# A head's first probability tile is transposed together with its second

## The chip, the cores and the metric

The kernel runs on one core of one Trainium2 chip. The metric is device time in microseconds (us) of one execution. Engines are called as in the profile: PE is TensorE's matmuls and PEld its weight loads, DVE is VectorE, ACT is ScalarE, POOL is GpSimd, SP is SyncE, which issues most DMAs.

## What is computed

Causal attention with a decay (4 batches, 8 heads, 576 rows, head size 64), then a small dense layer with a maximum over three products (moe1), then a routed layer of 8 experts, two per row. The change touches the attention alone:

```python
scores = scale * np.matmul(q, k.transpose(0, 1, 3, 2))
decay = cum[:, :, :, None] - cum[:, :, None, :]
scores = np.where(causal, -1000000000.0, scores + decay)
attn = np.exp(scores - np.max(scores, axis=-1, keepdims=True))
attn = attn / (np.sum(attn, axis=-1, keepdims=True) + 1e-09)
x = np.matmul(attn, v)
```

## The kernel before

Attention is cut into units: a batch's first 256 query rows (a short unit, tiles 0 and 1 of 128 rows) or its other 320 (a long unit, tiles 2, 3 and 4; tile 4 has 64 rows). A unit has 8 heads. The list `jobs` (lines 395 to 411) holds the 160 tiles in order: two per head in short units, three in long ones, there in the order 2, 4, 3 for heads of even number and 2, 3, 4 for odd ones. A tile is marked `first` or `last` within its head. The first 16 heads (a short and a long unit) are `plain`: their probabilities are used in one part. All later ones are split into a high and a low part, so that fp32 products can be made from faster ones.

A tile goes through these steps, each a function called from the loop in `attention()` (line 570): scores on TensorE (`st_S`, L446 or L448 and L449), mask, maximum and row minimum on VectorE (`st_max`, L457), exponential on ScalarE (`st_exp`, L462), division by the sum on VectorE and GpSimd (`st_norm`, L467, L468, L470), transposes on TensorE, one per 128 columns (`st_T`, L477), evacuation of the high part on ScalarE (`st_evac`, L489 or L503) and of the low part on VectorE (`st_evac2`, L510), and per head the product with V on TensorE (`st_pv`, L531 or L535) and its read-out (`st_x`, L547, or L550 and L551).

The loop is a pipeline written out by hand. Slot n has two halves. The first issues for ScalarE and VectorE: the evacuation of tile n-4, the exponential of n-1, the division of n-2, the maximum of n, the low part of n-4, the read-out of the head that ended with n-5. The second issues for TensorE: transposes of tile n-3, scores of tile n+1, the product with V of the head that ended with n-4. Engines run their queues in the order of issue, so this is the order of the work on each.

Between halves `att_to` (line 647) hands over to moe1 of the unit before: 22 groups a unit, of 12 or 18 matmuls (L661 to L663), whose results ScalarE and VectorE evacuate too (L681, L683, L687, L691, L712). These matmuls are what TensorE does while ScalarE and VectorE work on a tile. In the first unit, up to about 59 us, there are none yet. `post` (L730 to L856) routes the rows of a unit that moe1 is through with. After the last unit, from about 560 us, only the experts remain.

Buffers near the change: the transposes write to the PSUM tag `pt`, of which there are two; in long units the head's product with V takes its output `o` from the same two. Scores lie in `sA` (even tiles) or `sB` (odd ones, and the 64-row tile), one buffer each. Probabilities `P` are a ring of four.

Of the kernel before, what the change touches and what calls it, by code (L numbers as in the profile page):

```python
# [55 lines left out]
def moe_stack(ctx, tc, qk, v, f, w1, w2, w3, wo, wg, noise, e1, e2, out):  # L56
# [28 lines left out]
    with tc.manual_schedule():  # L85
# [113 lines left out]
        def load_v(b, ph, h):  # L199
            if hidx[b, ph, h] < H:  # L200
                if h % 2 == 0:
                    load_v_first(h)
                return
            vr = ap_.tile([128, 320], F32, tag="vr", name="vr", bufs=2).rearrange("p (j c) -> p j c", j=5)
            nj = 2 if ph == 0 else 4
            vh = v[b, :, h * D:(h + 1) * D]
            nc.sync.dma_start(vr[:, 0:nj, :], vh[0:nj * 128].rearrange("(j p) d -> p j d", p=128))
            if ph:
                nc.sync.dma_start(vr[0:64, 4, :], vh[512:576])
            vraws[b, ph, h] = vr  # L210
# [47 lines left out]
        def prep_v2(b, ph, h):  # L258
            if hidx[b, ph, h] < NV:
                return  # L260
            vr = vraws.pop((b, ph, h))
            s, pieces = v_pieces(b, ph, h)
            for pp, jj in pieces:
                nc.gpsimd.tensor_tensor(V[s][pp, jj, 64:128], vr[pp, jj, :],
                                        V[s][pp, jj, 0:64].bitcast(F32), op=OP.subtract)
# [130 lines left out]
        for b, ph in UNITS:  # L396
            for h in range(H):
                tiles = (0, 1) if ph == 0 else ((2, 4, 3) if h % 2 == 0 else (2, 3, 4))
                for n, i in enumerate(tiles):
                    t = Tile_()  # L400
# [50 lines left out]
        def st_max(t):  # L451
            st = ap_.tile([128, 4], F32, tag="stat", name="stat", bufs=6)
            t.st = st
            mk = maskw[0:t.w, MASK0 + t.w - t.kn:MASK0 + t.w]
            if t.i == 4:
                mk = mk.rearrange("p (a c) -> p a c", a=2)
            nc.vector.tensor_tensor_reduce(out=t.view, in0=t.view, in1=mk, scale=1.0, scalar=3.0e38,  # L457
                                           op0=OP.add, op1=OP.min, accum_out=st[0:t.w, 0:1])

        def st_exp(t):  # L460
            st = t.st
            nc.scalar.activation(t.pview, t.view, AF.Exp, bias=st[0:t.w, 0:1], scale=-1.0,  # L462
                                 accum_out=st[0:t.w, 1:2])

        def st_norm(t):
            st = t.st
            nc.vector.tensor_scalar(st[0:t.w, 2:3], st[0:t.w, 1:2], 1.0e-9, None, op0=OP.add)  # L467
            nc.vector.reciprocal(st[0:t.w, 3:4], st[0:t.w, 2:3])  # L468
            p = P[t.n % NP][0:t.w, 0:t.kn]
            nc.gpsimd.tensor_scalar(p, p, st[0:t.w, 3:4], 0.0, op0=OP.mult, op1=OP.add)  # L470

        def st_T(t):
            nb = t.i + 1
            p = P[t.n % NP]
            t.pt = ps_a.tile([128, 512], F32, tag="pt", name="pt", bufs=2)
            for j in range(nb):
                nc.tensor.transpose(t.pt[:, j * t.w:(j + 1) * t.w], p[0:t.w, j * 128:(j + 1) * 128],  # L477
                                    ident[0:t.w, 0:t.w])

        def st_evac(t):  # L480
            nb = t.i + 1
            hd = heads[t.b, t.ph, t.h]
            t.pl = None
            if t.plain:
                if t.first:
                    x = PT[t.h % 2]
                    hd["pf"] = x.rearrange("p (j c) -> p j c", j=5) if t.ph else \
                        x[:, 0:2 * QA_N].rearrange("p (j c) -> p j c", j=2)
                nc.scalar.activation(hd["pf"][:, 0:nb, t.c0:t.c0 + t.w],  # L489
                                     t.pt[:, 0:nb * t.w].rearrange("p (j c) -> p j c", j=nb), AF.Copy)  # L490
                return
            if t.first:
                if PT[0].dtype != F32R:
                    PT[:] = [ap_.tile([128, 5 * QB_N], F32R, tag=x, name=x) for x in ("PTh", "PTl")]
                if t.ph == 0:
                    o_ = (t.h % 2) * 2 * QA_N
                    hd["pt"] = [x[:, o_:o_ + 2 * QA_N].rearrange("p (j c) -> p j c", j=2) for x in PT]
                else:
                    hd["pt"] = [x.rearrange("p (j c) -> p j c", j=5) for x in PT]
            src = t.pt[:, 0:nb * t.w].rearrange("p (j c) -> p j c", j=nb)  # L500
            hh = hd["pt"][0][:, 0:nb, t.c0:t.c0 + t.w]
            ll = hd["pt"][1][:, 0:nb, t.c0:t.c0 + t.w]
            nc.scalar.activation(hh, src, AF.Copy)  # L503
            t.pl = (ll, src, hh)

        def st_evac2(t):
            if not t.pl:
                return
            ll, src, hh = t.pl
            nc.vector.tensor_tensor(ll, src, hh.bitcast(F32), op=OP.subtract)  # L510
# [27 lines left out]
        def st_x(t):  # L538
            hd = heads[t.b, t.ph, t.h]
            qn = SPAN[t.ph][1]  # L540
            o = hd["o"]
            r = (t.h % 2) * 64
            if r == 0:
                xf[0] = ap_.tile([128, QB_N], F32, tag="xf", name="xf")
            t.xf = xf[0]
            if t.plain:
                nc.scalar.activation(t.xf[r:r + 64, 0:qn], o[0:64, 0:qn], AF.Copy)  # L547
                return
            oc = ap_.tile([64, QB_N], F32, tag="oc", name="oc")
            nc.scalar.activation(oc[:, 0:qn], o[64:128, 0:qn], AF.Copy)  # L550
            nc.vector.tensor_tensor(t.xf[r:r + 64, 0:qn], o[0:64, 0:qn], oc[:, 0:qn], op=OP.add)  # L551
# [8 lines left out]
        def st_xl(t):  # L560
            if t.h % 2:
                qn = SPAN[t.ph][1]
                u, c = UNITS.index((t.b, t.ph)), t.h // 2
                XL[u, c] = mp.tile([128, QB_N], F32R, tag="xl", name="xl", bufs=XBUF)
                nc.gpsimd.tensor_tensor(XL[u, c][:, 0:qn], t.xf[:, 0:qn], XH[u, c][:, 0:qn].bitcast(F32),
                                        op=OP.subtract)
# [3 lines left out]
        def attention():  # L570
            NJ = len(jobs)

            def job(n):
                return jobs[n] if 0 <= n < NJ else None

            def nxt(t, d):
                k = hidx[t.b, t.ph, t.h] + d
                return hkey[k] if k < len(hkey) else None

            st_S(jobs[0])  # L580
            for n in range(NJT):
                now, last = job(n), lambda d: job(n - d) if job(n - d) and job(n - d).last else None
                if job(n - 4):
                    st_evac(job(n - 4))
                if job(n - 1):
                    st_exp(job(n - 1))
                if job(n - 2):
                    st_norm(job(n - 2))
                if now:
                    st_max(now)  # L590
                if job(n - 4):
                    st_evac2(job(n - 4))
                if last(6):
                    st_xl(last(6))
                if last(5):
                    st_x(last(5))
                tv = job(n - 3 - VSH)
                if tv and tv.first:
                    prep_v2(tv.b, tv.ph, tv.h)
                    k = nxt(tv, 2)  # L600
                    if k and (hidx[k] < H or hidx[k] >= NV + 2):
                        load_v(*k)
                yield
                if now and now.first and n and nxt(now, 1):
                    prep_head2(*nxt(now, 1))
                    k = hidx[now.b, now.ph, now.h]
                    if H <= k + AH < H + 3:
                        load_head(*hkey[k + AH])
                    if H + 3 <= k + 3 < len(hkey):
                        load_head(*hkey[k + 3])  # L610
                if job(n + 1) and job(n + 1).first and nxt(job(n + 1), 1):
                    prep_head(*nxt(job(n + 1), 1))
                tv = job(n - 2 - VSH)
                if tv and tv.first:
                    prep_v(tv.b, tv.ph, tv.h)
                if last(5):
                    st_xh(last(5))
                if job(n - 3):
                    st_T(job(n - 3))
                if job(n + 1):  # L620
                    st_S(job(n + 1))
                if last(4):
                    st_pv(last(4))
                    k = nxt(last(4), 2)
                    if k and H <= hidx[k] < NV + 2:
                        load_v(*k)
                yield
# [381 lines left out]
        n = 0  # L1009
# [233 lines left out]
```

## Time and profile before

| | |
|---|---|
| median of 3 runs | 1053.16 us (1051.28 to 1053.35) |
| profiled execution | 1053.1 us, span 1051.4 us |
| granted TensorE clock, mean | 0.995 |
| TensorE busy | 1010.5 us, 96% |
| VectorE busy | 537.7 us, 51% |
| ScalarE busy | 520.8 us, 50% |
| GpSimd busy | 487.9 us, 46% |
| probability transposes (L477) | 480, 76.7 us busy |

Busy time is from the page of the profile. TensorE's matmuls are pipelined and overlap, so its busy time isn't its time at full rate. What one costs is read from the starts of two that follow each other. In the timeline a row gives start, duration, engine, line, what is written and read, the count of merged instructions, and in brackets the idle time of the engine before it with what ended it.

### The profile page before, as it was taken

The numbers are of one execution on the slowest core, as the hardware profiler recorded it, in microseconds if no ns is written. First come the engines' busy times: TensorE is split into PE (matmuls) and PEld (weight loads), VectorE is DVE, ScalarE is ACT, GpSimd is POOL, SyncE is SP. The second block draws the span as 40 slices with busy tenths as digits, with TensorE's granted clock in tenths as the row PEclk, the third lists the DMA queues.
The fourth block names the chain that finished last, engine by engine and source line by source line (L and its number), as shares of the span: only waits on it lengthen the run. The fifth ranks groups of instructions, "written<-read, shape, count | busy, mean of one in ns | idle before, by whom it ended". The sixth has DMA issues, their size and how long they took to land.

```text
span 1051.4 us, 18712 instructions
## 1 busy us (share of the span) xinstructions
PE 1010.5 (96%) x6452; PEld 907.2 (86%) x6452; DVE 537.7 (51%) x1666; ACT 520.8 (50%) x1310; POOL 487.9 (46%) x573
## 2 busy tenths in 40 slices
PE   5899999999999999999999999999999999999996
PEld 3477798999989999999998889899898989898995
DVE  6989767587685876858363434222232322232210
ACT  5866766576665776666324244333333333333311
POOL 5766645545555555454345354443334342434202
PEclk9999999999999999999999999999999999999999
DMA  6875344332432213311025265543536353544203
GB/s 195 207 180 156 106 131 114 84 99 82 136 87 49 70 52 96 89 37 38 1 83 169 57 169 162 127 107 113 116 131 122 109 124 97 134 109 125 35 9 44
DMA packets 79728, 109.17 MB, mean 104 GB/s; under 512 B 37172, under 2 KB 43700, under 8 KB 79564
## 3 DMA queue, kind: packets, MB, share of 16 engines
q1 hardware_dynamic: 69388, 86.90, 28.8%
q0 software_dynamic: 10240, 21.02, 10.9%
q8 instruction: 53, 0.87, 0.4%
q14 instruction: 47, 0.39, 0.1%
HBM read 86.48 MB, written 21.39 MB: 103 GB/s over the span
## 4 chain that ended last, share of the span: by engine, by line
PE 78%; DVE 9%; DMA 5%; issue 3%; POOL 2%; ACT 2%; SPq 1%; POOLq 0%; DVEq 0%; ACTq 0%
PE m L661 8%; PE m L662 7%; PE m L663 7%; PE g L661 7%; PE g L662 7%; PE g L663 7%; PE m L974 6%; PE m L973 6%; PE m L972 6%; PE pt L477 4%; PE o L535 3%; PE o L531 2%; PE m L730 2%; PE t L938 2%; PE sB L448 1%
## 5 line engine op out<-in xcount | busy, mean ns | idle before, releaser
L470 POOL TENSOR_SCALAR P<-P,stat 128x512 f32<-128x512 f32 (+4 forms) x160 | 92.7, 579 | 206.4 <-DVE stat L468 117.3
L661 PE MATMUL g<-xTh,eh 128*128 128x384 f32 (+1 forms) x512 | 159.3, 311 | 0.6 <-DVE hl L957 0.6
L662 PE MATMUL g<-xTl,eh 128*128 128x384 f32 (+1 forms) x512 | 158.0, 309 | 0.0
L663 PE MATMUL g<-xTh,el 128*128 128x384 f32 (+1 forms) x512 | 157.9, 308 | 0.0
L979 POOL DMA_INDIRECT out_rows<-ys,dst x40 | 63.1, 1578 | 176.8 <-ACT ys L978 143.6
L309 POOL TENSOR_TENSOR el<-ew,eh 128x1024 fp32r<-128x1024 f32 x36 | 92.1, 2563 | 109.4 <-ACT eh L308 109.2
L957 DVE SCALAR_TENSOR_TENSOR hl<-g,hh 128x384 fp32r<-128x384 f32 (+1 forms) x120 | 58.2, 486 | 130.0 <-ACT hh L956 125.3
L972 PE MATMUL m<-eh,hh 128*128 128x512 f32 x296 | 118.8, 401 | 0.0
L974 PE MATMUL m<-eh,hl 128*128 128x512 f32 x296 | 117.1, 396 | 0.0
L956 ACT ACTIVATE hh<-g 128x384 fp32r<-128x384 f32 (+1 forms) x120 | 52.1, 435 | 130.9 <-PE g L663 130.6
L973 PE MATMUL m<-el,hh 128*128 128x512 f32 x296 | 116.8, 394 | 0.0
L941 DVE TENSOR_TENSOR xTl<-t,xTh 128x512 fp32r<-128x512 f32 x40 | 27.7, 692 | 157.1 <-ACT xTh L940 157.1
L978 ACT ACTIVATE ys<-m,mv 128x512 f32<-128x512 f32 x40 | 27.6, 689 | 161.1 <-issue 118.7
L661 PEld LDWEIGHTS g<-xTh,eh 128*128 128x128 f32 x512 | 96.7, 189 | 1.6 <-DVE hl L957 1.0
L662 PEld LDWEIGHTS g<-xTl,eh 128*128 128x128 f32 x512 | 96.8, 189 | 0.2 <-DVE xTl L941 0.2
L663 PEld LDWEIGHTS g<-xTh,el 128*128 128x128 f32 x512 | 96.7, 189 | 0.0
L503 ACT ACTIVATE PTh<-pt 128x128 fp32r<-128x128 f32 (+2 forms) x120 | 52.3, 436 | 77.7 <-PE pt L477 47.0
L477 PE MATMUL pt<-ident,P 128*128 128x128 f32 x480 | 76.7, 269 | 6.2 <-POOL P L470 4.6
L308 ACT ACTIVATE eh<-ew 128x1024 fp32r<-128x1024 f32 x64 | 67.4, 1055 | 8.5 <-DMA ew<-in_e 8.5
L974 PEld LDWEIGHTS m<-eh,hl 128*128 128x128 f32 x296 | 55.6, 188 | 13.2
L477 PEld LDWEIGHTS pt<-ident,P 128*128 128x128 f32 x480 | 53.0, 143 | 15.9 <-POOL P L470 8.8
L973 PEld LDWEIGHTS m<-el,hh 128*128 128x128 f32 x296 | 55.7, 188 | 11.9
(312 smaller groups left out, 2891.3 us busy)
## 6 DMA issues: line engine op xcount, KB each, us to landing
ew<-in_e SPq DMA_DIRECT2D x64, 512.0 KB
qkraw<-in_qk SPq DMA_DIRECT2D x64, 224.0 KB
wr<-in_w SPq DMA_DIRECT2D x18, 512.0 KB
qkraw<-in_qk SPq DMA_DIRECT2D x48, 128.0 KB
out_rows<-zt SPq DMA_DIRECT2D x19, 256.0 KB
vr<-in_v SPq DMA_DIRECT2D x37, 128.0 KB
x2d<-row SPq DMA_DIRECT2D x16, 256.0 KB
vr<-in_v SPq DMA_DIRECT2D x24, 64.0 KB
```

The source lines that it names most:

```text
L308: nc.scalar.activation(hi_, raw, AF.Copy)
L309: leng.tensor_tensor(lo_, raw, hi_.bitcast(F32), op=OP.subtract)
L470: nc.gpsimd.tensor_scalar(p, p, st[0:t.w, 3:4], 0.0, op0=OP.mult, op1=OP.add)
L477: nc.tensor.transpose(t.pt[:, j * t.w:(j + 1) * t.w], p[0:t.w, j * 128:(j + 1) * 128], ident[0:t.w, 0:t.w])
L661: nc.tensor.matmul(o, lh, rh, start=first, stop=False)
L662: nc.tensor.matmul(o, lh, rl, start=False, stop=False)
L663: nc.tensor.matmul(o, ll, rh, start=False, stop=last)
L957: nc.vector.scalar_tensor_tensor(hl, o, 0.0, hh.bitcast(F32), op0=OP.max, op1=OP.subtract)
L972: nc.tensor.matmul(y, hh, wh[:, f_ % 2, :], start=(f_ == 0), stop=False)
L973: nc.tensor.matmul(y, hh, wl[:, f_ % 2, :], start=False, stop=False)
L974: nc.tensor.matmul(y, hl, wh[:, f_ % 2, :], start=False, stop=(f_ == 7))
L979: nc.gpsimd.indirect_dma_start(out=out[:, :], out_offset=bass.IndirectOffsetOnAxis(ap=ex["dst"][:, e, c:c + 1], axis=0), in_=ys, in_offset ...
```

## The change

In the loop of `attention()` a head's first tile is transposed one slot later, in the slot of its second tile and right ahead of it. Its two evacuations are moved by one slot as well, so that both tiles of the pair are evacuated in the same half slot, the first one first: both high parts ahead of the exponential, both low parts behind the maximum. Third tiles, and the product with V, stay in their slots. Nothing else is changed.

```diff
                 now, last = job(n), lambda d: job(n - d) if job(n - d) and job(n - d).last else None
-                if job(n - 4):
-                    st_evac(job(n - 4))
+                turned = [t for t, d in ((job(n - 5), 5), (job(n - 4), 4)) if t and t.first == (d == 5)]
+                for t in turned:
+                    st_evac(t)
                 if job(n - 1):
                     st_exp(job(n - 1))
                 if job(n - 2):
                     st_norm(job(n - 2))
                 if now:
                     st_max(now)
-                if job(n - 4):
-                    st_evac2(job(n - 4))
+                for t in turned:
+                    st_evac2(t)
...
-                if job(n - 3):
-                    st_T(job(n - 3))
+                for t, d in ((job(n - 4), 4), (job(n - 3), 3)):
+                    if t and t.first == (d == 4):
+                        st_T(t)
                 if job(n + 1):
                     st_S(job(n + 1))
```

## Rows read from the trace of the kernel before

**Rows 1.** The page, busy time, share of the span and instructions of TensorE.
```profile
PE 1010.5 (96%) x6452; PEld 907.2 (86%) x6452; DVE 537.7 (51%) x1666; ACT 520.8 (50%) x1310; POOL 487.9 (46%) x573
```

**Rows 2.** Waits of TensorE: who waited for whom, us in total, times, longest.
```profile
PE pt L477 <- POOL P L470: 4.6, 3, 2.1
...
PE pt L477 <- DVE PTl L510: 1.5, 3, 0.6
...
PE sB L448 <- DVE xf L551: 1.4, 3, 0.5
```

**Rows 3.** Timeline of TensorE around runs of three and four 128-row transposes.
```profile
203.96 0.28 PE L663 MATMUL m<-xh,w00l 128*128 128x256 f32 x1
204.08 0.49 PE L477 MATMUL pt<-ident,P 128*128 128x128 f32 x3
204.32 0.37 PE L448 MATMUL sB<-QKB 128*64 128x288 f32 x1
204.54 0.29 PE L449 MATMUL sB<-QKA 128*64 128x288 f32 x1
204.67 0.29 PE L448 MATMUL sB<-QKB 128*64 128x288 f32 x1
...
210.05 0.60 PE L477 MATMUL pt<-ident,P 128*128 128x128 f32 x4
```

**Rows 4.** Timeline of TensorE where transposes of a 64-row tile begin.
```profile
218.93 0.28 PE L663 MATMUL m<-xh,w10l 128*128 128x256 f32 x1
219.13 0.52 PE L477 MATMUL pt<-ident,P 64*128 64x64 f32 x5
```

**Rows 5.** Timeline of TensorE at its idle times in the first long unit.
```profile
44.49 0.55 PE L477 MATMUL pt<-ident,P 128*128 128x128 f32 x3 [0.86 <-POOL P L470]
45.19 0.50 PE L448 MATMUL sA<-QKB 128*128 128x512 f32 x1 [0.15 <-ACT P L462]
...
49.96 0.37 PE L477 MATMUL pt<-ident,P 128*128 128x128 f32 x1 [2.12 <-POOL P L470]
```

**Rows 6.** Timeline of all engines ahead of a third tile's transposes, a later long unit.
```profile
220.47 0.76 DVE L457 CUSTOM_DVE_ANT_0 sB<-sB,maskw 64x576 f32<-64x576 f32 x1 [1.14 <-PE sB L449]
...
221.16 0.48 DVE L510 TENSOR_TENSOR PTl<-pt,PTh 128x320 fp32r<-128x320 f32 x1
...
221.58 0.38 PE L477 MATMUL pt<-ident,P 128*128 128x128 f32 x2
```

**Rows 7.** Timeline of all engines where a second tile's transposes wait.
```profile
227.78 0.54 DVE L510 TENSOR_TENSOR PTl<-pt,PTh 128x384 fp32r<-128x384 f32 x1
...
228.47 0.52 PE L477 MATMUL pt<-ident,P 128*128 128x128 f32 x3 [0.56 <-DVE PTl L510]
```

**Rows 8.** Timeline of all engines in a short unit, sixth head.
```profile
157.07 0.37 ACT L503 ACTIVATE PTh<-pt 128x256 fp32r<-128x256 f32 x1
...
157.48 0.27 PE L477 MATMUL pt<-ident,P 128*128 128x128 f32 x1
...
157.58 0.21 ACT L462 ACTIVATION_READ_ACCUMULATOR P<-sA,stat 128x1 f32 x1
...
157.84 0.45 PE L448 MATMUL sA<-QKB 128*128 128x384 f32 x1
```

**Rows 9.** Timeline where the product with V waits, seventh and first head.
```profile
165.02 0.41 DVE L510 TENSOR_TENSOR PTl<-pt,PTh 128x256 fp32r<-128x256 f32 x1
...
165.58 0.36 PE L535 MATMUL o<-PTh,V 128*128 128x256 f32 x1 [1.10 <-DVE PTl L510]
...
257.18 0.19 PEld L535 LDWEIGHTS o<-PTl,V 128*128 128x128 f32 x1 [0.23 <-DVE PTl L510]
```

**Rows 10.** Windows: busy us of PE, PEld, DVE, ACT, POOL, clock, DMA share, GB/s.
```profile
49.00:50.00 1.00, 0.04 (x1) 0.04 (x1) 1.00 (x4) 0.41 (x1) 0.81 (x2) 1.00 1.43 140
50.00:57.00 7.00, 6.14 (x19) 3.69 (x20) 6.80 (x18) 4.35 (x12) 5.32 (x6) 0.51 0.49 104
```

## The prediction, made before the changed kernel ran

> **What bounds the kernel now.** First the page: TensorE (PE) is busy 96% of the span and the next engine half of it, so the time is the length of TensorE's instruction stream plus its idle time [rows 1]. Next the view of waits, for TensorE alone, because a change of order can act only on what a view of waits shows or on what it newly creates: all of TensorE's waits for probabilities (pt from POOL) come to 4.6 us in three places [rows 2], so no more than that can be won by transposing a first tile later. Then the timeline of TensorE around a transpose run, to price the run itself [rows 3, 4], and the timeline of all engines at the places where the moved work stands close behind something [rows 5 to 9]. Last the clock by windows [rows 10].
>
> In what follows a head's tiles are its first, second and (in long units) third, and "slot" is one turn of the attention loop. The profiled execution took 1053.1 us (span 1051.4), the median of the runs is 1053.16, so sums are made on 1053.1.
>
> **The runs themselves.** The change removes no instruction. All 480 transposes stay; 64 heads have one run less each. What a run costs beyond its transposes: a run of three is shown with 0.49 us, a run of four with 0.60, so one transpose is 0.11 us. Three are 0.33, yet the score matmul behind them starts after 0.24 (204.08 to 204.32), 0.09 early. That score matmul takes 0.22 (204.32 to 204.54) against 0.13 for the next of the same form (204.54 to 204.67), 0.09 more: the two cancel. Before the run the last MoE matmul gives way after 0.12 us (203.96 to 204.08), which is its ordinary pitch [rows 3]. So a run of 128-row transposes costs its transposes and nothing for beginning or ending, and joining two runs saves about 0. The 64-row tile is different: the matmul before it gives way after 0.20 us (218.93 to 219.13), 0.08 more [rows 4]. In the 16 long heads with even number this tile now follows the first tile's transposes instead of a MoE matmul. No row shows these neighbours; between 0.08 saved and 0.08 more lost per head it is 16 times 0.08, 1.3 us either way. I take -0.3 for all runs together, near nothing, because the nearest row [rows 3] shows no price of transposing as such, only of the 64 rows.
>
> The Trainium skill, TensorEngine Tiling (Array Packing), section Key Properties, says that changing the tiling mode, as distinct from the tile, drains TensorE. The trace agrees as far as the 0.08 goes. By that rule going from 128-row to 64-row transposes drains as well and the sum for the runs would be 0; without it, -1.3.
>
> **The wait for probabilities that goes.** One of the three places is the first tile of a long head, which waits 0.86 us at 44.49. But the score matmul right behind it waits too, at 45.19, for an exponential on ScalarE, which waits for nothing of the transposes [rows 5]. Without the transposes in front the score matmul still starts at 45.19; the three transposes (0.33 us) leave an idle stretch and come back in a busy one. So this gain is 0, and the move costs up to 0.33 per place where a score matmul stands waiting so. In this first stretch most of it is taken up by the next idle time, 2.12 us at 49.96, which waits for another tile's probabilities [rows 5]. For the eight long heads without a low part: +0.4, bounds 0 and 2.6 (eight times 0.33).
>
> **New order in long heads (three tiles).** The two pt buffers turn, and in the new order the third tile's transposes need the buffer of the first. Before, the first tile was evacuated a slot and a half ahead of them; now its evacuation (ScalarE high part, VectorE low part) is in the half slot just ahead, and on VectorE behind that slot's max. The max waits for the scores, runs from 220.47, VectorE begins the low part at 221.16, and TensorE starts the next transposes at 221.58 [rows 6]. The low part that will stand there is that of a 384-wide tile, 0.54 us, and TensorE followed such a release 0.15 us after its end (228.32 to 228.47) [rows 7]. So 221.16 + 0.54 + 0.15 = 221.85, 0.27 us late. All of TensorE's queue stands behind it: the next scores and 12 MoE matmuls. I went through this place in all heads of the later long units: two of eight are late by 0.27 to 0.3, one by under 0.1, the others have more MoE or logit work between and are clear. Three units times 0.65 is +1.9 us; bounds 0 (VectorE relieved one slot earlier) and 24 times 0.27, 6.5. The first long unit has no low part and is left out.
>
> What is eased there: at 228.47 the second tile's transposes wait 0.56 us for the low part of the first [rows 7]; both now go in one run, on different buffers. The buffer of the second is then the one that the head's output left, and its evacuation, queued behind, ends about as late. Of three such waits, 1.5 us, I take -0.5.
>
> **New order in short heads (two tiles).** Both evacuations now fall in one slot, right before the head's P times V, and the exponential of that slot stands behind both on ScalarE. At 157.07 ScalarE evacuates a 256-wide tile in 0.37 us, the exponential's last part ends at 157.79 (157.58 + 0.21), and the scores start 0.05 later, with a transpose in their shadow at 157.48 [rows 8]. A second evacuation (128 wide, so under 0.37; I take 0.28) ahead of it moves the scores by 0.28, and the transpose, 0.11, comes back in the next slot: 0.39. In the next slot the scores wait up to 0.5 us anyway until VectorE has read this head's output out (three times, 1.4 us in all) [rows 2], which takes most of it: +0.1 each. The next head's P times V waits 1.10 us for VectorE's low part, from 165.02, at 165.58 [rows 9]; one more low part ahead of it (0.28) and one transpose out of the shadow (0.11) make +0.39. Both occur once in each of three units: 1.5 us. At the first head of two units P times V waits 0.23 for the same reason [rows 9], again +0.39 less what is slack: 0.3 each, 0.6. Sum +2.1; bounds 0.6 and 3.5. Elsewhere in these units the cover is over 1 us, the MoE matmuls.
>
> **What is moved past whom.** Only transposes and evacuations move. No DMA and no POOL instruction changes place; on ScalarE and VectorE one evacuation passes an exponential, a max and what the MoE issues in one slot. P is a ring of four, so the exponential that overwrites the first tile's P now follows its transposes by half a slot, but it already stands behind that slot's evacuation on ScalarE, which waits for later transposes: no new price.
>
> **The sum.** -0.3 + 0.4 + 1.9 - 0.5 + 2.1 = +3.6 us, 1053.1 + 3.6 = 1056.7 us. The measurement can tell about 0.2%, 2.1 us, from no change.
>
> **Rivals.**
> *Absorbed.* VectorE and ScalarE are half idle, and a slot without evacuation precedes each slot with two. If that head start is kept, the low parts come in time and only the shadows are lost: +0.4 + 0.6 - 0.5, about 1053.6. For it: the waits that exist are short [rows 2]. Against: in the places above VectorE starts its max only when the scores are done, so an earlier head start is lost there [rows 6].
> *Faster.* The clock. TensorE idles 2.12 us until 49.96 [rows 5], the granted clock is 1.00 up to 50 and 0.51 on the mean from 50 to 57 [rows 10], that is 1.2 instead of 2.4 GHz. The transposes moved away from 44.49 fill 0.33 us of the idle time there. If the clock then stays at 2.4 GHz, at most half of 7 us, 3.4, is won: with the sum above 1053.3, with the absorbed case 1050.2. It decides if the granted clock is 1.00 from 50 to 57. Against: the 0.86 us of 44.49 only changes its place, so TensorE is idle as long as before, and VectorE, busy for all of 49 to 50 and over 0.9 behind it [rows 10], would then set the pace there.
> *Slower by more.* The late third tile delays scores and by them the next max, so that the low part of the third tile and P times V are late too: twice 1.9, about 1058.6, at most 1061.
> *Not done as said.* If the pt buffer forced the second transposes apart from the first, runs would be split; the turn of two buffers lets both go when the output is out of the way, so I give it no chance of its own.
> The Trainium skill, TensorE: Matmul & The Clock Gate, Part 4: PE-mode transpose, says that transposes do not count as work for the clock gate as matmuls do. No row shows a fall of the clock behind transposes here; by that rule longer runs could cost, not save, and a second fall like that one would add 3.4 us [rows 10].
>
> **Chances.** Forecast (1055.3 to 1058) 0.38, slower by more 0.14, absorbed 0.26, faster 0.22. So by size: slower by over 0.2% 0.52, within 0.26, faster 0.22. The range of 8 in 10 reaches to the faster case and the slower one's end: 1050.2 to 1061.0. The likeliest case's own range is 1055.3 to 1058.
>
> **What will show it.** Right: in long heads third-tile transposes that wait for the low part (L510), 0.2 to 0.3 us, twice a unit; in short heads P times V idle at the unit's sixth and seventh head longer by 0.3 to 0.4; the first tile's wait for POOL gone while the scores behind start where they did. Wrong: a last MoE matmul ahead of scores, with no run between, at a pitch shorter than 0.12; a clock of 1.00 through 50 to 57; or waits of transposes for L510 no longer than the 1.5 us of before [rows 2].

## The result, and the profile after

The changed kernel took 1059.11 us (median of 5 runs, 1054.84 to 1059.71) against 1053.16 (1051.28 to 1054.24) for the kernel before on the same chip: a ratio of 1.0051, interval 1.0031 to 1.0071, slower by about 6 us. The profiled execution took 1059.11 us with a span of 1057.1, 5.7 us over the span of before.

The work is the same: on the page TensorE has as many instructions as in [rows 1] and stays at 96%.

```profile
PE 1012.9 (96%) x6452; PEld 907.8 (86%) x6452; DVE 542.1 (51%) x1666; ACT 519.1 (49%) x1310; POOL 487.9 (46%) x573
```

The view of TensorE's waits answers to [rows 2]. (Lines from L592 on have moved: L661 to L663 of before are L663 to L665 here, L938 is L940.)

```profile
PE sA L448 <- ACT P L462: 5.0, 8, 1.4
PE o L535 <- DVE PTl L510: 3.7, 3, 1.2
PE sB L448 <- ACT P L462: 2.9, 3, 2.1
PE t L940 <- DMA xg<-x2d,dst: 2.7, 1, 2.7
...
PE pt L477 <- DVE xf L551: 1.9, 3, 0.9
...
PE pt L477 <- POOL P L470: 1.4, 1, 1.4
PE pt L477 <- DVE PTl L510: 1.1, 5, 0.3
PE sB L448 <- DVE xf L551: 0.8, 3, 0.3
```

The change did what it says: transposes wait for POOL 1.4 us instead of 4.6. But new waits stand beside that: transposes for `xf`, the read-out of the output that held their buffer (1.9 us in three places, one in each later long unit); transposes for low parts in five places instead of three; and scores for the exponential, 5.0 and 2.9 us.

**Where the time comes in, by stages.** The start of each unit's first score matmul (L446 or L448) is in both timelines. A stage runs from one such start to that of the next unit; its change against the kernel before is the row below. Long and short units are those of the split probabilities, from 157.84 us of before on. "First stretch" is from the first scores to there, "gather" the stretch from the experts' 9th transpose (L938, L940) at 569.4 us to their 41st at 670.4, in which their first gathered rows come in. A long stage begins with the scores that stand behind the evacuations of a short unit's sixth head (157.84 of [rows 8]), so the delay of these scores is counted in the short stage, and what the short unit's last two heads lose in the long stage behind it.

| stage, start to end in before | changed | changed, again | before, again |
|---|---|---|---|
| first stretch, 8.61 to 157.84 | -0.4 | +1.2 | -0.3 |
| long, 157.84 to 241.38 | +1.30 | +1.32 | +0.01 |
| short, 241.38 to 287.06 | +0.42 | +0.62 | +0.02 |
| long, 287.06 to 370.57 | +1.35 | +1.35 | 0.00 |
| short, 370.57 to 416.28 | +0.60 | +0.60 | -0.03 |
| long, 416.28 to last scores 498.01 | +1.06 | +1.20 | +0.02 |
| last scores to gather, 498.01 to 569.4 | -0.7 | -0.7 | +0.3 |
| gather, 569.4 to 670.4 | +2.3 | +1.0 | -0.8 |
| the rest, 670.4 to the end | -0.2 | -0.5 | -0.6 |

The five unit stages repeat within 0.2 us from execution to execution. They give 4.7 and 5.1 us and are the change's price. The first stretch and the stages from the last scores on vary by more than that, and are looked at apart.

**A later long unit.** The timeline of the changed kernel in the first later long unit: the places of [rows 6] and [rows 7], and at 241.85 the second head of the kind that [rows 6] stand for.

```profile
220.22 0.76 DVE L457 CUSTOM_DVE_ANT_0 sB<-sB,maskw 64x576 f32<-64x576 f32 x1 [2.04 <-PE sB L449]
...
220.91 0.94 DVE L510 TENSOR_TENSOR PTl<-pt,PTh 128x384 fp32r<-128x384 f32 x2
...
221.17 0.28 PE L665 MATMUL m<-xh,w20l 128*128 128x256 f32 x1
...
221.60 0.63 PE L477 MATMUL pt<-ident,P 128*128 128x128 f32 x4 [0.15 <-DVE PTl L510]
...
227.29 0.76 DVE L457 CUSTOM_DVE_ANT_0 sB<-sB,maskw 64x576 f32<-64x576 f32 x1
...
227.46 0.49 PE L477 MATMUL pt<-ident,P 128*128 128x128 f32 x3
227.66 0.43 ACT L550 ACTIVATE oc<-o 64x320 f32<-64x320 f32 x1
...
228.20 0.48 DVE L551 TENSOR_TENSOR xf<-o,oc 64x320 f32<-64x320 f32 x1
...
228.83 0.63 PE L477 MATMUL pt<-ident,P 128*128 128x128 f32 x4 [0.87 <-DVE xf L551]
...
241.23 0.28 PE L665 MATMUL m<-xh,w02l 128*128 128x256 f32 x1
241.85 0.63 PE L477 MATMUL pt<-ident,P 128*128 128x128 f32 x4 [0.34 <-DVE PTl L510]
```

At 221.60 and 241.85 the third tile's transposes stand behind a max and a first low part, as forecast. At 228.83 the joined run is cut in two: its first three transposes go at 227.46, the other four wait until the read-out of the head's output, on VectorE behind the same max, has left their buffer.

A wait costs more than its bracket says. The bracket counts from the modelled end of the matmul ahead, 0.28 us after its start, while the next matmul of a stream starts 0.11 to 0.12 after it. At 221.60 the stream would have gone on at 221.17 + 0.11 = 221.28, so 0.32 us are lost, not 0.15; at 241.85 it is 0.51, not 0.34; at 228.83, with three transposes of 0.11 ahead, 1.04. Together 1.87 us. In the kernel before the one wait of this unit, 0.56 at 228.47 [rows 7], loses about 0.72 by the same count, from the start of the last matmul ahead:

```profile
227.63 0.28 PE L663 MATMUL m<-xh,w11l 128*128 128x256 f32 x1
```

The difference, 1.15, is nearly all of the stage's +1.30; the rest, 0.16, is the tail of the short unit, there by the first heads' scores. The second later long unit loses the same within 0.1. The last one has one late third tile (0.32) and 0.1 less at the second tile, and at its end the scores wait 1.4 us for an exponential, where they waited 0.6 before.

```profile
PE sA L448 <- ACT P L462: 1.4, 4, 0.6
```

(Waits of the kernel before; with the change 5.0, 8, 1.4, above.)

**A short unit.** The timeline of the changed kernel at the places of [rows 8] and [rows 9]:

```profile
156.46 0.54 ACT L503 ACTIVATE PTh<-pt 128x128 fp32r<-128x128 f32 x2
...
156.88 0.38 ACT L462 ACTIVATE P<-sA,stat 128x128 f32<-128x128 f32 x1
...
157.40 0.44 PE L448 MATMUL sA<-QKB 128*128 128x384 f32 x1 [0.47 <-ACT P L462]
...
164.59 0.61 DVE L510 TENSOR_TENSOR PTl<-pt,PTh 128x128 fp32r<-128x128 f32 x2
...
165.01 0.36 PE L535 MATMUL o<-PTh,V 128*128 128x256 f32 x1 [1.22 <-DVE PTl L510]
```

Two evacuations stand ahead of the exponential, and the scores at 157.40 wait for it with no transpose left to fill the gap. Two low parts stand ahead of the product with V. Counted by starts, in the next short unit the sixth head's scores come 2.72 us behind the scores ahead of them, before 2.44, so 0.28 is lost. The first head's product with V takes 0.73 us from its first matmul to its last, before 0.65, and the next scores are late by 0.2 to 0.3.

### The profile page after: what moved, and what is told of

It reads as the page before. It is cut to its first block, busy times and chain, and to the rows that moved or that the text cites. A ratio compares the mean times of both kernels' runs of the same rounds, so it can differ in the third digit from the quotient of the medians.

```text
span 1057.1 us, 18645 instructions
## 1 busy us (share of the span) xinstructions
PE 1012.9 (96%) x6452; PEld 907.8 (86%) x6452; DVE 542.1 (51%) x1666; ACT 519.1 (49%) x1310; POOL 487.9 (46%) x573
## 4 chain that ended last, share of the span: by engine, by line
PE 75%; DVE 13%; issue 3%; DMA 3%; POOL 2%; ACT 2%; SPq 1%; POOLq 0%; DVEq 0%; ACTq 0%
PE m L663 7%; PE m L665 7%; PE m L664 7%; PE g L663 6%; PE g L664 6%; PE g L665 6%; PE m L976 6%; PE m L975 6%; PE m L974 6%; PE pt L477 4%; PE o L535 3%; PE o L531 2%; DVE QKB L241 2%; PE m L732 2%; PE t L940 1%
## 5 line engine op out<-in xcount | busy, mean ns | idle before, releaser
L663 PE MATMUL g<-xTh,eh 128*128 128x384 f32 (+1 forms) x512 | 159.3, 311 | 0.6 <-DVE hl L959 0.6
L665 PE MATMUL g<-xTh,el 128*128 128x384 f32 (+1 forms) x512 | 157.9, 308 | 0.0
L663 PEld LDWEIGHTS g<-xTh,eh 128*128 128x128 f32 x512 | 96.7, 189 | 1.6 <-DVE hl L959 1.0
L665 PEld LDWEIGHTS g<-xTh,el 128*128 128x128 f32 x512 | 96.7, 189 | 0.0
L477 PE MATMUL pt<-ident,P 128*128 128x128 f32 x480 | 67.9, 267 | 5.2 <-DVE xf L551 1.9
L457 DVE CUSTOM_DVE_ANT_0 sB<-sB,maskw 128x256 f32<-128x256 f32 (+2 forms) x80 | 46.8, 585 | 49.1 <-PE sB L449 38.2
L503 ACT ACTIVATE PTh<-pt 128x128 fp32r<-128x128 f32 (+2 forms) x120 | 48.7, 435 | 47.0 <-PE pt L477 46.6
```

Source lines behind the costliest of these rows:

```text
L663: nc.tensor.matmul(o, lh, rh, start=first, stop=False)
L665: nc.tensor.matmul(o, ll, rh, start=False, stop=last)
```

## Experiments

Times with an interval are medians, with the ratio against the kernel before; times without are those of the profiled execution. "Later units" is the sum of the five unit stages of the table, from the profiled execution; it is what these experiments are read by, since it repeats within 0.5 us. The expectations name another measure, the start of the last probability transposes; that holds the first stretch as well, and two executions of the changed kernel differ by 2.0 us in it (512.9 and 514.9), so it can't tell the theories apart. For the first four runs, of one execution each, the kernel before took 1054.39 us alongside.

**The new order in short units alone** (for the transposes likewise, with `d == 4`).

```diff
-turned = [t for t, d in ((job(n - 5), 5), (job(n - 4), 4)) if t and t.first == (d == 5)]
+turned = [t for t, d in ((job(n - 5), 5), (job(n - 4), 4)) if t and (t.first and t.ph == 0) == (d == 5)]
```

> The new order in short units alone; long units as before. Measure: the start of the last probability transposes, 508.4 us before and 512.9 with the whole change (+4.5). Theory (waits for evacuations, sized by the trace of after: the later short units fall back by 0.2 to 0.6 us each, the first one by 0.8): +0.5 to +2. Rival (a joined run costs TensorE something by itself, the same for each of 64 heads): half of it, +2.2 or a little more, spread over the heads.

1055.19 us. The two later short stages cost 0.59 and 0.57, the long ones 0.14 to 0.19 each, nearly all of it at their start, where the short unit's last heads still run; later units +1.65.

**The new order in long units alone** (`t.ph == 1` in the same places).

> The new order in long units alone. Theory: the three later long units fall back by 1.0 to 1.3 us each, at the third tile's transposes behind the low part and at the second tile's behind the read-out of the head's output: +2.5 to +4, last transposes near 511.5 to 512.4. Rival (cost of a joined run): +2.2.

1055.48 us. The long stages cost 1.13, 1.19 and 0.92, the short ones 0.00 and 0.06; later units +3.30. With the run above 4.95, as much as the whole change (4.7 and 5.1): the prices of the two kinds of unit add. They are not the equal halves of the rival. The waits tell the causes apart: five for low parts and three for the read-out come with the long units alone.

```profile
PE pt L477 <- DVE xf L551: 2.0, 3, 0.9
...
PE pt L477 <- DVE PTl L510: 1.1, 5, 0.3
```

**First tile's low part ahead of the max**, the rest as changed.

```diff
+                for t in turned:
+                    if t.first:
+                        st_evac2(t)
                 if now:
                     st_max(now)
                 for t in turned:
-                    st_evac2(t)
+                    if not t.first:
+                        st_evac2(t)
```

> The whole change, but the low part of a first tile is issued ahead of that slot's max instead of behind it. Theory: TensorE's waits of transposes for the low part (L510), 1.1 us in five places, go; P times V's 3.7 us shrink by up to 0.6; the max and with it an exponential come up to 0.5 later where scores wait for them; last transposes 0.5 to 1.5 earlier than with the change, 511.4 to 512.4. Rival (run cost): 512.9 within 0.2.

1055.17 us; later units +2.3, the long stages 0.53, 0.51 and 0.74, the short ones 0.27 and 0.25. TensorE's list has no wait of transposes for L510 left, and the wait for the read-out stays.

```profile
PE o L535 <- DVE PTl L510: 3.4, 6, 0.6
...
PE pt L477 <- DVE xf L551: 1.7, 3, 0.7
```

So the low part behind the max is a part of the long units' price, about half, and the read-out is another.

**Only the evacuations moved, in short units**: every transpose where it was before, the first tile's evacuations one slot later (not in the last head of a unit).

```diff
+turned = [t for t, d in ((job(n - 5), 5), (job(n - 4), 4)) if t and (t.first and t.ph == 0 and t.h < 7) == (d == 5)]
-if job(n - 4):
-    st_evac(job(n - 4))
+for t in turned:
+    st_evac(t)
...
-if job(n - 4):
-    st_evac2(job(n - 4))
+for t in turned:
+    st_evac2(t)
```

> The kernel before, but in short units (all heads but a unit's last) the first tile's two evacuations are issued one slot later, together with the second tile's; transposes stay where they were, in two runs. Theory: the scores at a unit's sixth head and P times V at its seventh wait as with the change, so the later short units lose about what they lose there (0.2 to 0.6 us each) less the transpose that stays in the shadow (0.1 each): +0.3 to +1.5 at the last transposes. Rival (joined runs are the cost): 508.4 within 0.2.

1057.1 us; the two short stages cost 0.60 and 0.53, as in the changed kernel, and the long ones 0.38 to 0.42. But the transposes now wait for their buffers, six times, so this does not show by itself that the order of evacuation is the price.

```profile
PE pt L477 <- DVE PTl L510: 6.6, 6, 1.7
```

**Exponential ahead of both evacuations**, in the slots that evacuate a pair.

```diff
+if turned and turned[0].first and job(n - 1):
+    st_exp(job(n - 1))
 for t in turned:
     st_evac(t)
-if job(n - 1):
+if job(n - 1) and not (turned and turned[0].first):
     st_exp(job(n - 1))
```

> The changed kernel with the exponential ahead of the two evacuations on ScalarE in each slot that evacuates a pair. Theory: in short units the second evacuation in front of the exponential delays the scores; turned round, the scores' waits for ScalarE (L448 for L462, 5.0 and 2.9 us in the changed kernel) fall back to about 1.5 and 1.9 us, but the evacuations end 0.5 to 0.8 us later, so the product with V waits longer for the low part (3.7 us in the changed kernel, to 5 us or more) and in long units the third tile's low part comes no earlier: in all between 1.5 us less and 1 us more than the changed kernel, 1057.5 to 1060 us. Rival: the evacuations are what is late everywhere, and the exponential has slack; then the waits for the low part double in short and long units, and the time is over 1061 us.

1060.2 us, ratio 1.0068 (1.0056 to 1.0080): in all as slow as the changed kernel. The stages tell it apart: the short ones fall to 0.01 and 0.17, the long ones rise to 1.98, 2.03 and 1.95, later units +6.1. The sixth head's scores now come 2.30 us behind the scores ahead of them instead of 2.72: their delay is the evacuation in front of the exponential. But the price does not go, it moves by one slot. The second scores of a long stage, still beside the short unit's seventh head, are later by 0.7 us than in the changed kernel, for the read-out; in the first two long stages this is all of the rise, and behind it the long heads lose what they lose with the change (1.1). Neither of the two expected outcomes was the whole of it.

```profile
PE o L535 <- DVE PTl L510: 4.4, 5, 1.3
```

Timeline at the second scores of the first later long unit:

```profile
162.92 0.35 PE L448 MATMUL sB<-QKB 128*64 128x288 f32 x1 [0.56 <-DVE xf L551]
```

**Read-out ahead too**: the first tile's low part ahead of the max, as in the run of that name (its lines are left out below), and the head's read-out ahead of exponential and max.

```diff
                     st_evac(t)
+                if last(5):
+                    st_x(last(5))
                 if job(n - 1):
                     st_exp(job(n - 1))
...
-                if last(5):
-                    st_x(last(5))
```

> The whole change, the low part of a first tile ahead of the max (as in the run before, which brought the last transposes from 512.9 to 510.0), and the read-out of a head's output ahead of that slot's exponential and max. Theory (waits for evacuations): the second tile's waits for the read-out, 1.7 us in three places, go to under 0.4; the scores' waits for the read-out at a unit's seventh head, 1.4 us, go as well; the max and exponential come later where scores wait for them, so 1 to 2.5 us in all: 507.5 to 509.0. Rival (a joined run costs by itself): not below 509.5.

1067.23 us, ratio 1.0145 (1.0128 to 1.0161); later units +12.1. The wait of transposes for L551 is gone, and the kernel is slower for it. Argued from the order, not shown apart: the read-out needs the product with V, stands in ScalarE's and VectorE's queues until that is done, and holds back the exponential, the max and the low parts behind it. The product with V waits thirteen times.

```profile
PE o L535 <- DVE PTl L510: 7.4, 13, 0.9
```

**Kernel before, low part ahead of the max** in every slot, nothing joined.

```diff
-                if now:
-                    st_max(now)
                 if job(n - 4):
                     st_evac2(job(n - 4))
+                if now:
+                    st_max(now)
```

> The kernel before, with the low part ahead of the max in every slot and nothing else. Theory (VectorE's order behind the scores sets these waits, whichever slot transposes stand in): the waits of transposes (1.5 us) and of P times V (3.3 us) for the low part shrink to under 1.5 together; scores wait more for exponentials, by up to 1.5; last transposes 505.5 to 508.0. Rival: the order on VectorE does not matter without joined runs: 508.4 within 0.3.

1049.61 us (1047.01 to 1051.50), ratio 0.9965 (0.9953 to 0.9977): faster than both kernels. Later units -3.2: the long stages -1.09, -1.05 and -0.67. The 1.5 us of waits for L510 of [rows 2] are gone from the list, and those of the product with V fall to 1.1 us.

```profile
PE o L535 <- DVE PTl L510: 1.1, 3, 0.4
```

**Changed kernel, both low parts ahead of the max**: the same order on VectorE as in the run above, but joined.

> The changed kernel with both low parts of a pair (and that of a third tile) ahead of the slot's maximum on VectorE: the order of the kernel before with its low part ahead of the maximum, which took 1049.6 us, but with the first tile's transposes joined to the second's. Theory: the price of joining is the place of the evacuations in the in-order queues. With VectorE's order mended the transposes wait for low parts (L510) no more, the three later long units cost nothing or gain up to 0.5 us each as in that kernel, and only ScalarE's order in the short units is left, 0.2 to 0.6 us a unit: starts of scores from the second batch to the last move by -2 to +0.5 us against the kernel before, and the time is 1050.5 to 1053.5 us. Rival: joining itself costs, because the second tile's buffer is the one that the head's output leaves, so that transposes wait for its read-out (xf, L551) whatever stands behind; the same stretch is then +2 to +3 us, as with the first tile's low part alone in front, and the time is 1055 to 1057 us.

1054.74 us (1051.24 to 1057.71), ratio 1.0016 (1.0005 to 1.0027). Later units -0.2 against the kernel before, so the theory's stretch came out; its time did not, by 1.2 us; the gather stage is +2.1 in the profiled execution, with a fall of the clock in it (3.4 us from 607.42). But against the run above, with VectorE in the same order, joining costs 3.0 us of the later units and 5.1 us of the median. In the first later long unit, where joining costs 0.84, the waits show the join's own part:

```profile
PE pt L477 <- DVE xf L551: 0.5, 1, 0.5
```

This is the only wait of TensorE from 170 to 250 us, 0.69 us by starts, and the unjoined kernel has none there. So theory and rival both hold in part: the low part behind the max was a removable half of the price, and the read-out that the second half of a joined run waits for is the join's own.

The short stages, +0.04 and +0.03, are not free of the change either. The sixth head's scores wait as in the changed kernel, 2.71 us behind the scores ahead, and the first head's product with V takes 0.35 us instead of 0.73. So ScalarE's order sets the one and VectorE's order the other, and here they cancel.

```profile
158.39 0.44 PE L448 MATMUL sA<-QKB 128*128 128x384 f32 x1 [0.47 <-ACT P L462]
```

**Both kernels again.**

> The changed kernel once more, for a second trace and for more times with their clocks. Theory: up to the last probability transposes the trace repeats, 512.9 within 1 us; what comes behind (the wait for the first gathered rows, 2.66 us, and a fall of the clock at 611) is not the change's and differs: a wait between 1 and 3.5 us, and no fall of the clock behind it in some executions. Rival (the later place of everything brings wait and fall about): both are there again, at 610 to 612.

> The kernel before once more, for a second trace. Theory: last probability transposes at 508.4 within 1 us; idle time ahead of the first gathered rows other than the 0.73 and 1.30 us of the first trace, or a fall of the clock at another place. Rival: these too repeat within 0.2 us.

1059.0 us, ratio 1.0056 (1.0044 to 1.0068), and 1051.72. The stages are in the table. The last transposes of the changed kernel are 2.0 us later than in its first execution, outside the 1 us expected; 1.6 of it is the first stretch. The wait for the gathered rows is there again, and no fall of the clock behind it. The early fall of the clock is no mark of either kernel. The granted clock is half for 6.8 us from 50.12 in the kernel before, for 3.4 us from 55.02 in the changed kernel, and in these two it is 6.8 us from 51.78 (changed) and 3.4 from 53.64 (before). The first stretch varies with it: from -1.6 to +2.8 us over all executions, in no order by kernel. It can be charged neither to the change nor against it.

**The gather stage.** The one wait of 2.66 us for the experts' first gathered rows is in both executions of the changed kernel (2.7 and 2.7); in the kernel before there are two, of at most 1.3. It follows from the last scatter of `meta` (L854, L852 before), whose landing SP's next read waits for. Timeline of the changed kernel:

```profile
599.95 0.89 POOL L854 DMA_INDIRECT meta<-mt,sli  x1 [0.23 <-issue]
604.05 0.81 SPq L917 DMA_DIRECT2D mv<-meta  x2
...
606.35 0.98 POOL L932 DMA_INDIRECT xg<-x2d,dst  x1 [5.22 <-DVE dst L925]
...
610.44 0.66 PE L940 MATMUL t<-ident,xg 128*128 128x128 f32 x4 [2.66 <-DMA xg<-x2d,dst]
```

Its DMA view from 600.2 to 604.5 us (a queue with packets, MB and share; an issue with median us to landing):

```profile
q8 instruction: 1, 0.02, 2.9%
...
meta<-mt,sli POOLq DMA_INDIRECT x1, 4.1
```

In the kernel before, the same scatter is followed by SP's read 2.2 us later:

```profile
596.34 0.90 POOL L852 DMA_INDIRECT meta<-mt,sli  x1 [0.21 <-issue]
598.53 0.81 SPq L915 DMA_DIRECT2D mv<-meta  x2
```

The line "q8 instruction" is a fetch of program code: one packet of 16384 bytes, from 0.69 to 2.71 us behind the scatter's issue; 60 of the scatter's 64 packets have moved by then, its last four move from 2.69 on. Queue 8 has 53 such packets (0.87 MB on the page). From one to the next TensorE goes through 254 of its records (matmuls, weight loads and waits; the median in the kernel before). The changed kernel has 46 fewer waits on TensorE (278 against 324; over all engines 18645 records against 18712), so the same fetch comes later against the work: 4.87 us ahead of the scatter's issue in the kernel before, 0.69 behind it in the changed one. In the other orders of the attention it comes later with fewer waits of TensorE as well (312: 3.2 us ahead; 300: 2.15 ahead; 274: 0.9 behind). Two runs place it on purpose, with tiny matmuls in TensorE's first idle stretch that are used for nothing, 32 in the changed kernel and 94 in the kernel before:

```diff
+pad = [ps_m.tile([128, 512], F32, tag="m", name="pad") for _ in range(3)]
+for _ in range(32):
+    nc.tensor.matmul(pad[0][0:32, 0:32], onesb[:, 0:32], onesb[:, 0:32], start=True, stop=True)
 st_S(jobs[0])
```

> The changed kernel with 32 tiny matmuls (32x32, result unused) in TensorE's first idle stretch, which ends at 8.60 us: 64 more TensorE instructions, so the fetches of its instructions (queue 8, 53 packets of 16384 bytes) come about 5 us earlier against the work. In the changed kernel one of them started 0.69 us behind the issue of the last scatter of meta and took 2.0 us, and the scatter landed 4.1 us after its issue; now it should start about 4 to 5 us ahead of it, as in the kernel before (4.87). Theory: that fetch holds the scatter back, and the wait of the first gathered rows (xg) follows from it. Then the longest such wait falls from 2.7 to about 1.3 us, the part from the end of attention to the last expert is shorter by 1 to 2.5 us, and the time is 1056.5 to 1058 us. Rival: the wait comes from the attention's delay, or from the gather itself; then it stays at 2.7 and the time at 1059.

1057.84 us, ratio 1.0043 (1.0028 to 1.0057). The fetch came 6.51 us ahead of the scatter, the scatter landed in 2.1 us, and the wait went back to what it was before. Later units +4.7, as without the shift; the gather stage -0.7 instead of +2.3 and +1.0. But the stretch ahead of it, last scores to gather, is +0.7 instead of -0.7: a wait of moe1's matmuls for ScalarE, 1.1 us, is there again that the kernel before has (0.6) and the changed one has not.

```profile
PE t L943 <- DMA xg<-x2d,dst: 1.4, 2, 0.7
```

Its DMA view from 600 to 604 us:

```profile
meta<-mt,sli POOLq DMA_INDIRECT x1, 2.1
```

> The kernel before with 94 such matmuls in the same idle stretch: 188 more TensorE instructions, which with a fetch of 256 instructions amounts to each fetch 68 instructions later, as the changed kernel has it (67 fewer). Theory: a fetch then starts 0.4 to 1.5 us behind the last scatter, its landing takes 3.5 to 4.5 us instead of 2.2, the longest wait for xg grows from 1.3 to between 2.2 and 3, and the time grows by 1 to 2.5 us to 1054 to 1055.5 us though the attention is as it was. Rival: no such wait appears, or it appears and the experts take it up later; then 1053 us.

The fetch came 2.84 us behind the scatter, later than meant. That fits the count above: the 67 records fewer of the expectation are those of all engines, and TensorE has only 46 fewer. It hit the next transfer: the read of `meta`, 2.62 us long instead of 0.81. The wait of 2.6 appeared with the attention unchanged.

```profile
599.50 2.62 SPq L918 DMA_DIRECT2D mv<-meta  x2
...
607.55 0.66 PE L941 MATMUL t<-ident,xg 128*128 128x128 f32 x4 [2.62 <-DMA xg<-x2d,dst]
```

But the median is 1052.1 us, ratio 0.9998 (0.9987 to 1.0009): no time lost that can be measured. So the place of the fetch and the wait it makes are shown in both directions. In the fourteen profiled executions the gather stage is +0.9 to +2.6 us in the seven where a fetch starts 0.4 to 2.9 us behind the scatter, and -0.8 to 0.0 in the others. In four of the seven (+1.6 to +2.6) the clock falls for 3.4 us behind the wait, in the other three (+0.9 to +1.6) it does not. What it is worth in the time is not settled: 1.2 us by medians in the changed kernel, with intervals that overlap, and nothing in the kernel before. Taken from the last scores to the gather's end the fetch costs little where the clock stays up: +0.3 in the repeat of the changed kernel against 0.0 with the shift, +0.1 in the shifted kernel before. The +1.6 of the first execution holds the fall of the clock at 611.39.

## Why the prediction was right, and where its steps failed

The direction was right, and the time, 1059.11, lies in the range and 2.4 us over the forecast of 1056.7. By stages the five later units cost 4.7 to 5.1 us where the sum had +3.1 for them: 1.4 for the long heads (1.9 - 0.5) and 1.7 for the short ones (2.1, less 0.4 for the third unit's sixth head, which lies in the first stretch). The short units alone measured 1.65, the long ones alone 3.30. So what the sum lacked lies in the long heads. The gather, with the stretch ahead of it +0.3 to +1.6, was not in the sum. That no more than 2.4 us is missing has something of chance: one term had the wrong sign, and how much the stages beside the attention add differs from execution to execution.

- **Runs, -0.3.** Right that joining is worth nothing. In a long head of even number the joined run of eight takes 0.87 us to the scores behind it (218.46 to 219.33). Apart, five 64-row transposes take 0.42 (212.17 to 212.59) and start 0.25 behind the matmul ahead, 0.13 beyond its pitch of 0.12; three take 0.24 and lengthen the score matmul behind by 0.09 [rows 3]; 0.88 in all. The change from 128-row to 64-row transposes inside the run costs about as much as the one it replaces: 0.20 us from start to start, where two of 128 rows are 0.11 apart. The Trainium skill, TensorEngine Tiling (Array Packing), section Key Properties, says that a change of tiling mode drains TensorE; the trace agrees with it between transposes as well.

```profile
211.92 0.28 PE L665 MATMUL m<-xh,w20l 128*128 128x256 f32 x1
212.17 0.50 PE L477 MATMUL pt<-ident,P 64*128 64x64 f32 x5
212.59 0.45 PE L448 MATMUL sB<-QKB 128*128 128x384 f32 x1
...
218.46 0.94 PE L477 MATMUL pt<-ident,P 128*128 128x128 f32 x8
219.33 0.35 PE L448 MATMUL sB<-QKB 128*64 128x288 f32 x1
```

- **The wait for POOL, +0.4.** Its mechanism is there: the scores behind 44.49 now wait 1.25 us for the exponential, at 45.90, instead of 0.15 [rows 5]. Its size can't be read beside the clock's fall.

```profile
45.90 0.50 PE L448 MATMUL sA<-QKB 128*128 128x512 f32 x1 [1.25 <-ACT P L462]
```

- **Third tile behind the low part, +1.9.** Right in place, cause and size. Priced by the ends it was 0.65 a unit; by the starts of the stream it is 0.32 + 0.51 = 0.83 in two units and 0.32 in the last, 2.0 in all. That a low part first takes it away shows the cause.
- **Second tile eased, -0.5.** This is the step that failed. It named the right buffer, the one that the head's output left, but took what frees it to end "about as late" as the low part. The read-out goes through ScalarE and then VectorE, behind the max, and ends at 228.68, where the low part ended at 228.32 [rows 7]. So the wait is not eased but longer in two of the three later long units, 1.04 us lost instead of 0.72 in the unit shown, and 0.1 shorter in the last: +0.5 in all where -0.5 stood. Of the 1.9 us that the sum lacked in long units this is 1.0; another 0.4 is the last unit's scores that wait for the exponential, which had no term; the rest was not placed.
- **Short heads, +2.1.** Right in cause and in size, as the short units alone show (1.65 for 1.7). Its parts: the first head's product with V 0.2 to 0.3 (0.3 forecast); the sixth head's scores 0.28 (0.39 forecast, its 0.28 for the evacuation exact). The seventh head's product with V waits 1.22 instead of 1.10, not 0.39 more, because its scores and so its max had come earlier (low parts from 164.59, before from 165.02), and with the slack in the scores' wait for the read-out (0.3 us instead of 0.5) the tail comes to 0.16, where the forecast left 0.1.
- **Rivals.** "Slower by more" is nearest in size, and its mechanism is not what happened: the product with V waits 3.7 us instead of 3.3. "Absorbed" is out by the unit stages. "Faster" hung on the clock from 50 to 57 us. It was 0.86 in the profiled execution, and the fall of full length came again in the next one: it differs by execution, not by kernel. As to the rule that transposes do not count for the clock gate (the Trainium skill, TensorE: Matmul & The Clock Gate, Part 4: PE-mode transpose), no fall in the later units of the changed kernel came with the joined runs of eight. (The run with the read-out ahead has three falls there, behind idle times of 0.7 to 0.9 us.) The falls of the profiled execution stand behind idle times of 2.08 us (to 53.67) and 2.66 us (to 610.44).

```profile
50.00:57.00 7.00, 4.39 (x17) 2.37 (x18) 6.80 (x19) 4.40 (x11) 5.54 (x7) 0.86 0.56 66
...
611.00:615.00 4.00, 4.00 (x15) 3.16 (x14) 0.69 (x1) 0.60 (x1) 1.35 (x2) 0.57 0.72 131
```

(Windows, columns as in [rows 10].)

- **Not seen.** "No DMA changes place" was true of the kernel's transfers and not of the fetches of its program.
- **The signs.** One sign of being wrong came true without the prediction being so: waits of transposes for L510 "no longer than the 1.5 us of before" are 1.1 us. The third tile's new waits are those 1.1; the 1.5 of before, the second tile's, have changed their name to `xf` and are 1.9.

Still open: 0.5 us of the long units' price, and what the fetches and the falls of the clock are worth in the time.

## What to carry to other kernels

On an engine that runs its queue in order, a step that is put off lands behind whatever is issued in its new slot: price it by that, and the buffer of the second half of a joined run by the last reader of what lay in it, not by the reader that is waited for now. Look first for a wait that a swap of two neighbours in a queue removes: low part ahead of max, two lines, won 3.3 us where the move of the transposes lost 6. And read a change by stages that repeat between executions, since those that don't can be as large as the effect.

## What the runs showed of the hardware that was not expected

- A fetch of program code (16384 bytes in one packet) takes 0.9 to 2.9 us and can hold back small transfers: a scatter's last packets moved only when the fetch had ended, and it landed 4.1 us after its issue instead of 2.1 to 2.2; a read took 2.62 us instead of 0.81. Its place moves with the number of TensorE's instructions, waits included: 46 records fewer put it 5.6 us later, 64 more put it 7.2 us earlier.
- The clock falls for 3.4 or 6.8 us behind idle times of TensorE in some executions and not in others, and the length of the idle time does not tell which: falls came behind 0.7 us (read-out ahead, 264.5 us) as behind 2.66 us (changed kernel, 611.4), and none came behind 2.73 us in the second execution of the changed kernel or behind 3.05 us in the run with the first low part ahead.
